# Budgets of the top-k rounds, a parallel first group, spread zero stores and a separate queue for the last gate's stores in a fused attention and expert kernel

## The chip, the cores and the metric

The kernel runs on one core of a Trainium2 chip. The engines are TensorE (PE, with its weight loads PEld), VectorE (DVE), ScalarE (ACT), GpSimd (POOL) and SyncE (SP, which here only issues DMAs); each works through its own instructions in order. The metric is the device time of one execution in microseconds, lower is better.

## What is computed

Attention over 8 batches, 12 heads, 448 positions and head size 64, with q and k normalised by their root mean square, feeds a layer of 8 experts in which every expert keeps its 80 strongest tokens. Cut to what matters:

```python
q_n, k_n = rmsnorm(q, g_q), rmsnorm(k, g_k)      # x / sqrt(mean(x*x) + 1e-6) * g
attn = softmax(q_n @ k_n.T / 8)
x = (attn @ v).transpose(0, 2, 1, 3).reshape(3584, 768)
logits = x @ w_gate                               # 768 x 8
expert_idx, probs = argmax(logits), softmax(logits)
gate_w = probs[arange(N), expert_idx]
for e in range(8):
    tok_idx = where(expert_idx == e)              # the 80 with the largest gate_w
    h = maximum(x[tok_idx] @ w1[e], 0)            # 768 x 1024
    out[tok_idx] = gate_w[tok_idx, None] * (h @ w2[e])   # other rows of out stay zero
```

## The kernel before

**Attention.** The heads are taken in 24 groups of four (three groups to a batch), each group in 7 steps, and two steps make a slot: 84 slots, of about 5 us each, numbered from 0; the slots from -10 prepare the first groups. In a slot PE makes the scores of two steps (L309, and L302 for the 64 left-over positions of each head), ACT takes their exponentials (L311), and PE multiplies those of the slot before with v (L331, L324). DVE adds up the exponentials of a half group in `presum` (L343, L345, L347, L350, all into `sm`), and PE turns the sums and the raw outputs into softmax denominators and gate logits in `zl` (L364, L368), four slots after the group's first. The order of all of this is written out by hand: `at_slot` hangs a step on the beginning, the middle or the end of a slot, and every engine follows that order.

**Preparation of a group.** `load_qk` fetches q and k ten slots ahead on SP's queue, into a ring of five buffers; `square` (ACT, L240), `rstd` (sums on DVE, L249 and L250, then the power -0.5 on POOL, L253), `normalise` (POOL, L263 and L269; DVE for the first two groups) and `transp` (PE, L276 and L281, then the ACT copies L289 and L291) follow. For group 0 this is done in four passes, q and k by two halves each, one pass to a slot from -10 on, each pass whole before the next. Ten matmuls on zeros (`wps`, L810) run on PE ahead of them.

**Gate and top-k.** At the end of batch b, `gate1`, `gate1v`, `gate2` and `gate2b` make the gate weights `gw`, and SP stores them (tile `rg`) to the scratch rows in DRAM, L426 and L429. For batches 0 to 3 together, the 80 best of each expert are found by 10 rounds of DVE's max, index and replace (L475 to L478) on 128 rows of 448 values, and 10 rounds more on 8 rows of 320. The rounds lie in `queue`; at the end of each slot `work(us)` adds its budget to `credit` and takes rounds from the queue while `credit` is above zero, each round charged with `cost`. When the last round is done the token numbers are fetched (`numbers`, POOL), and `close` appends to `first`.

**Merges.** Batches 4 to 7 are ranked in themselves (`rank_in_batch`, L542 to L582) and then merged one after the other into the running 80 best (`merge`): p0 (PE transposes the expert choice, L597, ACT copies it to `eqT`), p1 (PE, L605, with `aval`, ACT copies to `own`), v1 (DVE), p2 (PE, L625, ACT `move`), v2 and v3 (DVE `keep`, `put`), p3 (PE, L651 and L655, ACT `ainfo`), p4 (PE, L663, ACT writes `aval`, which the next merge needs). For batches 4 to 6 `chain_step` hangs these on half slots, no merge before `first` is set; the merge of batch 7 stands behind the loop.

**Zero rows.** 28 stores of zeros to the output (L799) stand on SP's queue, one in each slot from 6 to 33.

**Experts.** Behind the loop SP loads the weights of experts 3 to 5 (L172), POOL gathers the chosen rows (L866), and each expert runs L883, L900, L904, L915, L918 and a scatter (L923). The last batch's `rg` stores stand on SP's queue behind the six weight loads, and the first gather waits for them and for the token numbers `idxT` (L858).

Of the kernel before, what the change touches and what calls it, by code (L numbers as in the profile page):

```python
# [20 lines left out]
def kernel(  # L21
# [50 lines left out]
    nc.scalar.activation(warm[:, 0:1], warm[:, 1:2], AF.Exp)  # L72
# [5 lines left out]
    for half in range(2):  # L78
        nc.scalar.dma_start(out=gk2[half * D:(half + 1) * D, 0:1], in_=g_q[:, None])
        nc.scalar.dma_start(out=gk2[half * D:(half + 1) * D, 1:2], in_=g_k[:, None])  # L80
    gqk = cpool.tile([128, 1], F32, name="gqk")
    nc.vector.tensor_mul(gqk[:, :], gk2[:, 0:1], gk2[:, 1:2])
    nc.vector.tensor_scalar_mul(gqk[:, :], gqk[:, :], 1.0 / math.sqrt(D))
    zsb = cpool.tile([128, 512], F32, name="zsb")
    nc.gpsimd.memset(zsb[:, S:], 1.0)
# [19 lines left out]
    nc.vector.memset(nhalf[:, :], -0.5)  # L105
    ZW = 192
# [79 lines left out]
    with tc.tile_pool(name="qk", bufs=5) as qkpool, \  # L186
# [56 lines left out]
        def rstd(g, a, parts=ALLB):  # L243
# [8 lines left out]
            for lo, hi in parts:  # L252
                nc.gpsimd.tensor_tensor(rs[:, lo:hi], ms[:, lo:hi], nhalf[:, lo:hi], op=ALU.pow)  # L253
# [128 lines left out]
        def gate1v(b):  # L382
# [3 lines left out]
            rg = gpool.tile([128, NT, H + 1], F32, tag="rg", name="rg")  # L386
# [26 lines left out]

        def gate2x(b):
            nc.scalar.activation(gst[b]["lex"][:], gst[b]["lex"][:], AF.Exp)

        def gate2b(b):
# [4 lines left out]
            gw = gpool.tile([128, NT], F32, tag="gw", name="gw", bufs=4)  # L422
            nc.vector.reciprocal(gw[:], lsum[:])
# [5 lines left out]
            nc.sync.dma_start(out=xr_dram[b * S + SM:(b + 1) * S, DM:XW],  # L429
                              in_=rg[:SR, NJ])  # L430
            gwb = gw[:].unsqueeze(2).to_broadcast([128, NT, E])
# [11 lines left out]
        def gate2i(b):  # L443
# [5 lines left out]
            if b == B - 1:  # L449
                nc.gpsimd.memset(info[:], 0.0)  # L450
# [18 lines left out]
        def rounds(get, rows, width, val):  # L469
# [9 lines left out]
            cost = (3 * (width + 60) / 960 + 0.3, )  # L479
# [3 lines left out]
        def lists(val, idx):  # L483
# [9 lines left out]
            return [(0.0, go)]  # L493
# [37 lines left out]
        def rank_in_batch(b, hidden):  # L531
# [53 lines left out]
            return [(0, p1, v1, 4.0), (6, p2, v2, 0.4)]  # L585

        def merge(b, hidden):
# [26 lines left out]
            def v1():  # L614
                m["ahead"] = tpool.tile([128, NT, CAP], BF16, tag="ahead", name="ahead")
                nc.vector.tensor_tensor(m["ahead"][:], m["own"],
                                        m["gw"][:].unsqueeze(2).to_broadcast([128, NT, CAP]),
# [30 lines left out]
            def p3():  # L648
                ps = scps.tile([128, 2, 512], F32, tag="sc", name="mp")
# [105 lines left out]
        for g in range(NG):  # L755
# [24 lines left out]
            if g % NQ == NQ - 1:  # L780
# [8 lines left out]
                if b >= NB0:  # L789
                    at_slot(begins, b0 + 7, gate2i, b)  # L790
# [172 lines left out]
```

## Time and profile before

| | us |
|---|---|
| three runs: median (lowest to highest) | 580.26 (579.28 to 582.1) |
| the profiled execution, its own time | 581.99 |
| its span, first to last instruction | 580.3 |
| PE busy | 506.0 (87%) |
| DVE busy | 340.6 (59%) |
| ACT busy | 313.7 (54%) |
| POOL busy | 297.0 (51%) |

Mean granted clock of TensorE 0.922 of full speed. The shares are means over very different stages: up to about 38 us PE waits for the first groups; from there to about 486 us it works almost without a break, except between 270 and 400 us; from 490 to 530 us it runs at half clock and mostly waits, and then the experts follow. Where PE is busy throughout, work taken off it shortens the time; where it waits, the row that names the releaser tells what would.

### The profile page before, as it was taken

The page shows a single profiled execution, that of the slowest core. Times are in us where ns is not written, and L with a number is a line of the kernel's source. Part 1 is how long each engine was busy: PE and PEld are TensorE (multiplying, and loading weights), DVE is VectorE, ACT ScalarE, POOL GpSimd, SP SyncE. Part 2 cuts the span into 40 slices and gives each one's busy share as a digit, 9 for nine tenths or more (in the row PEclk, how much of TensorE's full clock was granted, in tenths as well). Part 3 has the DMA queues.
Part 4 walks back from the last instruction along what each step waited for, and adds up shares of the span by engine and source line. Part 5 has one row for each costly group of instructions (what it writes and reads, how often), then busy time and mean ns, then how long its engine had stood idle before and what let it go on. Part 6 is the DMA issues. An engine that isn't in the chain of part 4 may idle for free. (4 is left out here: it accounts for less than half of the span.)

```text
span 580.3 us, 9011 instructions
## 1 busy us (share of the span) xinstructions
PE 506.0 (87%) x3325; PEld 228.2 (39%) x3325; DVE 340.6 (59%) x588; ACT 313.7 (54%) x521; POOL 297.0 (51%) x221
## 2 busy tenths in 40 slices
PE   5389999999998999999888999989999998415795
PEld 4133334433333333443223333424435444314674
DVE  2364476464843665379897899494765625502442
ACT  2456776767665676676564664755775633000111
POOL 3479285775955749467175186468781000102231
PEclk8679999999998999999997998999999988556999
DMA  6438989899999969957673496745585500794942
GB/s 168 115 100 168 208 261 219 247 241 255 232 222 275 229 150 198 182 140 157 161 161 77 128 174 125 176 128 89 152 168 89 119 2 32 301 384 129 386 128 69
DMA packets 107531, 100.72 MB, mean 174 GB/s; under 512 B 29152, under 2 KB 99296, under 8 KB 106208
## 3 DMA queue, kind: packets, MB, share of 16 engines
q1 hardware_dynamic: 90736, 70.76, 40.8%
q0 software_dynamic: 15872, 29.14, 28.5%
q8 instruction: 26, 0.43, 0.3%
q10 hardware_dynamic: 880, 0.26, 0.2%
q14 instruction: 17, 0.14, 0.1%
HBM read 101.12 MB, written 39.91 MB: 243 GB/s over the span
## 5 line engine op out<-in xcount | busy, mean ns | idle before, releaser
L253 POOL TENSOR_TENSOR rs<-ms,nhalf 128x14 f32<-128x14 f32 (+2 forms) x52 | 148.6, 2861 | 141.8 <-DVE ms L250 127.9
L311 ACT ACTIVATE at<-ps 128x896 f32<-128x896 f32 x144 | 125.9, 915 | 36.5 <-PE ps L309 18.0
L309 PE MATMUL ps<-qkT 64*128 64x448 f32 x576 | 134.3, 579 | 0.0
L331 PE MATMUL po<-at,vt 128*64 128x448 f32 x576 | 127.3, 557 | 0.0
L249 DVE TENSOR_REDUCE ms<-sq 128x14 f32<-128x896 f32 (+2 forms) x52 | 52.6, 1012 | 87.6 <-ACT sq L240 87.3
L289 ACT ACTIVATE qkT<-tp,gqk 128x448 f32<-128x448 f32 (+2 forms) x72 | 34.1, 508 | 81.3 <-PE tp L281 69.3
L263 POOL TENSOR_TENSOR qn<-qk,rs 128x768 f32<-128x768 f32 x44 | 74.9, 1702 | 0.2
L276 PE MATMUL tp<-ident,qn 128*128 128x128 f32 x288 | 53.8, 297 | 18.9 <-DVE qn L263 16.1
L309 PEld LDWEIGHTS ps<-qkT 64*128 64x128 f32 x576 | 49.3, 189 | 48.3 <-issue 38.4
L343 DVE TENSOR_TENSOR sm<-at 128x896 f32<-128x896 f32 x48 | 57.1, 1189 | 15.1 <-ACT at L311 15.0
L276 PEld LDWEIGHTS tp<-ident,qn 128*128 128x128 f32 x288 | 31.2, 145 | 82.1 <-issue 63.1
L350 DVE TENSOR_TENSOR sm<-sm,at 128x896 f32<-128x896 f32 x48 | 54.7, 1140 | 1.5
L331 PEld LDWEIGHTS po<-at,vt 128*64 128x64 f32 x576 | 34.0, 136 | 54.6 <-issue 52.3
L240 ACT ACTIVATE sq<-qk 128x896 f32<-128x896 f32 (+2 forms) x52 | 46.6, 904 | 3.3 <-DMA gk<-in_g_k_dram 3.3
L364 PE MATMUL zl<-sm,zsel 128*32 128x448 f32 x192 | 33.3, 592 | 11.9 <-DVE sm L350 11.7
L904 ACT ACTIVATE h_sb<-ph 128x320 bf16<-128x320 f32 x16 | 7.0, 437 | 63.3 <-PE ph L900 63.3
L291 ACT COPY qkT<-tp 128x448 f32<-128x448 f32 (+2 forms) x72 | 27.2, 412 | 24.6 <-PE tp L281 24.4
L354 ACT COPY us<-po 128x448 f32<-128x448 f32 x48 | 25.7, 534 | 16.6 <-PE po L324 11.9
L368 PE MATMUL zl<-us,wgs 128*32 128x448 f32 x192 | 33.7, 600 | 0.0
L347 DVE TENSOR_TENSOR sm<-sm,ar 64x896 f32<-64x896 f32 x24 | 30.2, 1258 | 5.4 <-ACT ar L311 4.9
L680 PEld LDWEIGHTS xp<-ident,us 128*128 128x128 f32 x192 | 20.8, 144 | 31.3 <-issue 29.9
L345 DVE TENSOR_TENSOR sm<-sm,ar 64x896 f32<-64x896 f32 x24 | 32.1, 1337 | 0.8
(151 smaller groups left out, 555.2 us busy)
## 6 DMA issues: line engine op xcount, KB each, us to landing
wb_scratch<-in_moe_w_dram POOLq DMA_DIRECT2D x10, 1536.0 KB, 13.9
w_sb<-wb_scratch SPq DMA_DIRECT2D x10, 1536.0 KB, 18.6
out_dram<-zeros SPq DMA_DIRECT2D x28, 384.0 KB, 4.1
vt<-in_v_dram SPq DMA_DIRECT2D x24, 384.0 KB, 7.4
w_sb<-in_moe_w_dram POOLq DMA_DIRECT2D x6, 1536.0 KB, 15.9
xr_scratch<-xb SPq DMA_DIRECT2D x24, 384.0 KB, 4.5
qk<-in_q_dram SPq DMA_DIRECT2D x23, 384.0 KB, 4.6
qk<-in_k_dram SPq DMA_DIRECT2D x23, 384.0 KB, 4.5
```

What stands on the lines that cost most here:

```text
L240: nc.scalar.activation(st[g]["sq%d" % a][:, lo:hi], st[g]["qk"][a][:, lo:hi], AF.Square)
L249: nc.vector.reduce_sum(out=ms[:, lo:hi], in_=st[g]["sq%d" % a][:, lo:hi], axis=AX.X)
L253: nc.gpsimd.tensor_tensor(rs[:, lo:hi], ms[:, lo:hi], nhalf[:, lo:hi], op=ALU.pow)
L263: eng.tensor_mul(qn[:, :M].rearrange("p (j h) d -> p h j d", h=4)[:, h0:h1], qk[:, h0 * NJ:h1 * NJ].rearrange("p (h j) d -> p h j d", j=NJ ...
L276: nc.tensor.transpose(tp[:, j * 128:(j + 1) * 128], qn[:, 4 * j + 2 * u:4 * j + 2 * u + 2].rearrange("p h d -> p (h d)"), ident[:, :])
L289: nc.scalar.activation(o, x, AF.Copy, scale=gqk[:, :])
L309: nc.tensor.matmul(ps[:, hh, :S], T1[d, u, j * 128:(j + 1) * 128], T0[d, u, :], start=True, stop=True)
L311: nc.scalar.activation(at[:], ps[:, :, :S], AF.Exp)
L331: nc.tensor.matmul(st[g]["po%d" % u][hh * D:(hh + 1) * D, :S], vt[:, (2 * u + hh) * NJ + j, :], at[:, hh, :], start=(x == 0), stop=(x == R ...
L343: nc.vector.tensor_add(sm[:], s["at%d" % (x - 1)][:], s["at%d" % x][:])
L350: nc.vector.tensor_add(sm[:], sm[:], s["at%d" % x][:])
L368: nc.tensor.matmul(t[32 * c:32 * c + 32, :S], wgs[:, 4 * i + c, :], st[g]["us%d" % (c // 2)][:, :], start=False, stop=(i == NQ - 1))
```

## The change

Seven edits; the line numbers of the changed kernel are some 5 to 35 higher.

1. Budgets: a round is charged 0.25 us more, `work` adds 2.0 instead of 2.2 us a slot, a ranking is charged 4.6 instead of 4.0, and the gate steps, which were charged nothing, take 2.8 and 1.0 us off the credit (`spent`). A ranking also waits for `listed`, set when the first ten rounds are done and stored.
2. Group 0: both squares, then both `rstd`, then both `normalise` of a half, in three slots; the first half's `rstd` is ACT's square root and DVE's reciprocal instead of POOL's power. The table that holds the exponential is loaded behind it. The gains g_q and g_k are loaded behind k instead of ahead of it. 22 matmuls on zeros instead of 10.
3. Zero stores: from slot 4 on, spread over slots 4 to 78.
4. Buffers: q/k ring 4 instead of 5, `sm` 4 instead of 3, `rg` 4 instead of 2; `gw` is a column of `rg`, which removes a POOL copy.
5. Last gate: its `rg` stores go to ACT's queue; the clearing of `info` on POOL is gone.
6. Last merge: p3 makes only the token number, half as many columns.
7. Matmuls without use (`busy`) on PE ahead of the last merge, behind its p2 and behind its p3: 40, 40 and 70. The clearing of the gather buffers stands further back.

```diff
-    nc.scalar.activation(warm[:, 0:1], warm[:, 1:2], AF.Exp)
+    nc.scalar.activation(warm[:, 0:1], warm[:, 1:2], AF.Sqrt)
...
-    with tc.tile_pool(name="qk", bufs=5) as qkpool, \
+    with tc.tile_pool(name="qk", bufs=4) as qkpool, \
...
             for lo, hi in parts:
-                nc.gpsimd.tensor_tensor(rs[:, lo:hi], ms[:, lo:hi], nhalf[:, lo:hi], op=ALU.pow)
+                if parts is HALF[0]:
+                    nc.scalar.sqrt(rs[:, lo:hi], ms[:, lo:hi])
+                    nc.vector.reciprocal(rs[:, lo:hi], rs[:, lo:hi])
+                else:
+                    nc.gpsimd.tensor_tensor(rs[:, lo:hi], ms[:, lo:hi], nhalf[:, lo:hi],
+                                            op=ALU.pow)
...
-                s["sm%d" % u] = sm = prep.tile([128, 2, S], F32, tag="psm", name="sm", bufs=3)
+                s["sm%d" % u] = sm = prep.tile([128, 2, S], F32, tag="psm", name="sm", bufs=4)
...
+        def spent(us):
+            credit[0] -= us
...
-            nc.gpsimd.tensor_copy(rg[:, :, H], gw[:])
-            nc.sync.dma_start(
+            eng = nc.sync if b < B - 1 else nc.scalar
+            eng.dma_start(
...
-            if b == B - 1:
-                nc.gpsimd.memset(info[:], 0.0)
...
-            cost = (3 * (width + 60) / 960 + 0.3, )
+            cost = (3 * (width + 60) / 960 + 0.55, )
...
-            credit[0] = min(credit[0] + us, us)
+            credit[0] = min(credit[0], 0.0) + us
...
+            if which == "r" and not listed:
+                return False
...
-                        t = -10 + 2 * x + a
+                        t = -10 + 4 * x
                         at_slot(mid, t, square, g, a, HALF[x])
-                        at_slot(mid, t, rstd, g, a, HALF[x])
-                        at_slot(mid, t, normalise, g, a, HALF[x])
+                        at_slot(mid, t + 1, rstd, g, a, HALF[x])
+                        at_slot(mid, t + 2, normalise, g, a, HALF[x])
...
+                at_slot(end, b0 + 6, spent, 2.8)
+                at_slot(end, b0 + 7, spent, 1.0)
...
-            at_slot(begins, 6 + i, lambda i=i: nc.sync.dma_start(
+            at_slot(begins, 4 + 11 * i // 4, lambda i=i: nc.sync.dma_start(
...
-        for i in range(10):
+        for i in range(22):
             nc.tensor.matmul(wps[:, i % 2, :ZW], zeros[:, :128], zeros[:, :], start=True, stop=True)
...
-            work(2.2 if s < NS else 9)
+            work(2.0 if s < NS else 9)
...
+    def busy(n):
+
+        for i in range(n):
+            nc.tensor.matmul(hot[:, :128], identb[:, :], identb[:, :], start=True, stop=True)
...
+    busy(40)
     gate2(b)
```

What the edits move is shown at three places, first DVE at the start, group 0 (`ms` the mean squares, `rs` their inverse roots, `qn` the normalised q or k). Before, q's first half, up to the next pass:

```order
L249 TENSOR_REDUCE ms<-sq 128x6
L250 TENSOR_SCALAR ms<-ms 128x6
L249 TENSOR_REDUCE ms<-sq 128x2
L250 TENSOR_SCALAR ms<-ms 128x2
L119 CAST tabF<-tabI 8x1
L76 CAST identb<-ident 128x128
L263 TENSOR_TENSOR qn<-qk,rs 128x2x3x64
L269 TENSOR_TENSOR qn<-qk,rs 128x128
```

The sums of k begin behind this. Of the change, from the last sum of q's first half on, the same place on DVE:

```order
L254 TENSOR_SCALAR ms<-ms 128x2
L259 RECIPROCAL rs<-rs 128x6
L259 RECIPROCAL rs<-rs 128x2
L253 TENSOR_REDUCE ms<-sq 128x6
L76 CAST identb<-ident 128x128
L123 CAST tabF<-tabI 8x1
L254 TENSOR_SCALAR ms<-ms 128x6
```

k's sums now stand ahead of q's `normalise`, so that q and k go through the chain together.

Second, DVE at the first rounds of top-k, in slot 46 and the slot behind it (`R` the 448 gate weights of a row, `v` the eight largest). Before:

```order
L475 MAX v_162<-R 128x8
L476 MAX_INDEX idx<-v_162,R 128x8
L478 MATCH_REPLACE R<-v_162,R 128x448
L475 MAX v_162<-R 128x8
L476 MAX_INDEX idx<-v_162,R 128x8
L478 MATCH_REPLACE R<-v_162,R 128x448
L343 TENSOR_TENSOR sm<-at 128x896
L350 TENSOR_TENSOR sm<-sm,at 128x896
```

Of the change:

```order
L485 MAX v_156<-R 128x8
L486 MAX_INDEX idx<-v_156,R 128x8
L488 MATCH_REPLACE R<-v_156,R 128x448
L352 TENSOR_TENSOR sm<-at 128x896
L359 TENSOR_TENSOR sm<-sm,at 128x896
```

One round stands in the slot instead of two. By the budgets' arithmetic the twenty rounds take slots 46 to 62 before and 46 to 73 now, `close` comes in slot 81 instead of 70, and the merges of batches 4, 5 and 6 take slots 82 to 90 instead of 71 to 85; the last scores are those of slot 83.

Third, ACT at the end, from the copy of the last batch's logits (`zsb`) to the experts. Before, with the merge of batch 6 in the first rows and that of batch 7 in the last:

```order
L373 COPY zsb<-zl 128x448
L659 COPY ainfo<-mp 80x16
L664 COPY aval<-mp 8x80
L684 COPY xb<-xp 128x4x128
L415 ACTIVATE lex<-lex 128x32
L600 COPY eqT<-mp 8x512
L628 ACTIVATE move<-mp,rowF 80x8
L904 ACTIVATE h_sb<-ph 128x320 x16
```

Of the change, where the merge that ends at the top is batch 4's:

```order
L382 COPY zsb<-zl 128x448
L670 COPY ainfo<-mp 80x16
L675 COPY aval<-mp 8x80
L695 COPY xb<-xp 128x4x128
L610 COPY eqT<-mp 8x512
L621 COPY own<-mp 128x320
L638 ACTIVATE move<-mp,rowF 80x8
...
L427 ACTIVATE lex<-lex 128x32
L610 COPY eqT<-mp 8x512
L438 DMA xr_scratch<-rg 384x1x13
```

Two whole merges (batches 5 and 6) now stand behind the last batch's logits, where none began before.

## Rows read from the trace of the kernel before

**Rows 1.** Waits of PE, whole span: us in total, times, longest
```profile
PE zl L364 <- DVE sm L350: 11.7, 5, 4.6
```

**Rows 2.** Timeline at the start: start us, busy us, engine, line, [idle before <-releaser]
```profile
1.79 6.55 PE L810 MATMUL wps<-zeros 128*128 128x192 f32 x20 [1.79 <-DVE zeros L108]
...
6.24 0.72 ACT L240 ACTIVATE sq<-qk 128x384 f32<-128x384 f32 x2 [3.32 <-DMA gk<-in_g_k_dram]
...
9.06 2.04 POOL L253 TENSOR_TENSOR rs<-ms,nhalf 128x6 f32<-128x6 f32 x2 [5.60 <-DVE ms L250]
...
11.07 0.64 PE L276 MATMUL tp<-ident,qn 128*128 128x128 f32 x3 [2.73 <-DVE qn L263]
...
22.09 3.22 PE L309 MATMUL ps<-qkT 64*128 64x448 f32 x8
...
30.98 0.87 PE L276 MATMUL tp<-ident,qn 128*128 128x128 f32 x3 [4.34 <-DVE qn L263]
```

**Rows 3.** Stretches: length, busy us of each engine, granted clock, DMA share, GB/s
```profile
200.00:250.00 50.00, 49.18 (x300) 19.35 (x298) 26.12 (x35) 35.82 (x57) 25.99 (x17) 1.00 0.87 188
...
300.00:305.00 5.00, 2.10 (x12) 0.35 (x8) 4.76 (x11) 1.89 (x3) 2.61 (x1) 0.99 1.10 208
305.00:310.00 5.00, 3.26 (x13) 0.70 (x14) 4.93 (x9) 0.00 (x0) 2.03 (x1) 0.50 0.92 203
...
350.00:355.00 5.00, 5.00 (x28) 1.34 (x20) 4.83 (x12) 1.57 (x3) 4.32 (x2) 0.73 0.27 69
...
380.00:395.00 15.00, 12.15 (x63) 4.01 (x61) 13.20 (x26) 6.76 (x11) 9.03 (x6) 0.89 0.35 93
```

**Rows 4.** Timeline of DVE, the first two rounds of top-k
```profile
263.96 0.62 DVE L475 MAX8 v<-R 128x8 f32<-128x448 f32 x1
...
266.06 0.63 DVE L475 MAX8 v<-R 128x8 f32<-128x448 f32 x1
```

**Rows 5.** Groups of DVE, 260 to 310 us: count, busy us, mean ns, idle before
```profile
L343 DVE TENSOR_TENSOR sm<-at 128x896 f32<-128x896 f32 x5 | 9.7, 1932 | 0.0
```

**Rows 6.** Timeline at 176 us, ACT
```profile
176.69 0.58 ACT L684 COPY xb<-xp 128x512 f32<-128x512 f32 x1 [2.44 <-DMA xr_scratch<-xb]
```

**Rows 7.** Timeline of PE, steps p1 and p3 of a merge among the attention
```profile
444.72 1.11 PE L605 MATMUL mp<-aval,eqT 8*128 8x80 f32 x8
...
465.98 0.74 PE L651 MATMUL mp<-info,put 128*80 128x16 f32 x8 [0.26 <-ACT at L311]
466.57 1.29 PE L655 MATMUL mp<-ainfo,keep 80*80 80x2 f32 x16
```

**Rows 8.** Timeline of the end, from the last logits to the experts
```profile
484.09 1.28 PE L364 MATMUL zl<-sm,zsel 128*32 128x448 f32 x8
...
486.05 0.32 PE L625 MATMUL mp<-eqb,ahead 128*80 128x8 bf16 x4
...
491.73 0.21 ACT L664 COPY aval<-mp 8x80 f32<-8x80 f32 x1 [0.92 <-PE mp L663]
...
494.40 1.01 PE L597 MATMUL mp<-ident,eq 128*8 128x128 f32 x4 [1.86 <-DVE eq L411]
...
496.07 1.99 PE L605 MATMUL mp<-aval,eqT 8*128 8x80 f32 x8 [0.66 <-ACT eqT L600]
...
496.88 3.09 SPq L172 DMA_DIRECT2D w_sb<-wb_scratch  x6
...
510.17 0.16 DVE L858 CAST idxT<-mp 80x8 uint32<-80x8 f32 x1 [3.52 <-PE mp L655]
...
524.03 1.05 POOL L866 DMA_INDIRECT xg<-xr_scratch,idxT  x1 [24.05 <-DMA xr_scratch<-rg]
...
529.68 3.36 PE L900 MATMUL ph<-xgT,w_sb 128*128 128x80 bf16 x48 [0.50 <-DVE xgT L886]
...
536.04 1.88 PE L900 MATMUL ph<-xgT,w_sb 128*128 128x80 bf16 x48
```

**Rows 9.** Waits of SP's queue, 10 to 480 us: us in total, times, longest
```profile
SPq L204 <- POOL qn L269: 5.0, 3, 3.2
```

More of the change, by code (lines that the diff above doesn't have):

```diff
@@ L77, with load_g, gains @@
     gk2 = cpool.tile([128, 2], F32, name="gk2")
-    for half in range(2):
-        nc.scalar.dma_start(out=gk2[half * D:(half + 1) * D, 0:1], in_=g_q[:, None])
-        nc.scalar.dma_start(out=gk2[half * D:(half + 1) * D, 1:2], in_=g_k[:, None])
     gqk = cpool.tile([128, 1], F32, name="gqk")
[L82 to L85, printed above, removed]
+    def load_g():
+        for half in range(2):
+            nc.scalar.dma_start(out=gk2[half * D:(half + 1) * D, 0:1], in_=g_q[:, None])
+            nc.scalar.dma_start(out=gk2[half * D:(half + 1) * D, 1:2], in_=g_k[:, None])
+    def gains():
+        nc.vector.tensor_mul(gqk[:, :], gk2[:, 0:1], gk2[:, 1:2])
+        nc.vector.tensor_scalar_mul(gqk[:, :], gqk[:, :], 1.0 / math.sqrt(D))
     zsel = cpool.tile([128, NQ, 32], F32, name="zsel")
@@ L105 @@
     nc.vector.memset(nhalf[:, :], -0.5)
+    zsb = cpool.tile([128, 512], F32, name="zsb")
+    nc.gpsimd.memset(zsb[:, S:], 1.0)
     ZW = 192
@@ L385, in gate1v @@
             ztv = zt[:, :].rearrange("p (j c r) -> p j r c", j=NT, c=4)
[L386 removed]
+            rg = gpool.tile([128, NT, H + 1], F32, tag="rg", name="rg", bufs=4)
             rz = rg[:, :, :H].rearrange("p j (i c) -> p j i c", c=4)
@@ L697 @@
         v03 = tpool.tile([128, CAP], F32, name="v03")
-        first, queue, queue2, merging = [], [], [], []
+        first, listed, queue, queue2 = [], [], [], []
         r, ix = rounds(lambda: gst[0]["R"], 128, S, v03)
@@ L797 @@
         at_slot(begins, 0, load_wgs)
+        at_slot(begins, -10, load_g)
+        at_slot(end, -9, gains)
+        at_slot(mid, -8, lambda: nc.scalar.activation(warm[:, 0:1], warm[:, 1:2], AF.Exp))
         for i in range(N // 128):
-            at_slot(begins, 6 + i, lambda i=i: nc.sync.dma_start(
+            at_slot(begins, 4 + 11 * i // 4, lambda i=i: nc.sync.dma_start(
                 out=out[i * 128:(i + 1) * 128, :].rearrange("p (c f) -> p c f", f=ZW),
@@ L838 @@
         fetch_late(e)
-    xgs, xts, gws = {}, {}, {}
-    for e in range(3):
-        xgs[e] = mpool.tile([CAP, XW], F32, tag="xg", name="xg", bufs=3)
-        nc.gpsimd.memset(xgs[e][:, :], 0.0)
+    hot = tpps.tile([128, 512], F32, tag="tp", name="hot")
+    def busy(n):
+        for i in range(n):
+            nc.tensor.matmul(hot[:, :128], identb[:, :], identb[:, :], start=True, stop=True)
     b = B - 1
@@ L854 @@
     rp1()
-    for f in (v1, rv1, p2, rp2, v2, rv2, v3, p3):
-        f()
+    v1()
+    rv1()
+    p2()
+    busy(40)
+    rp2()
+    v2()
+    rv2()
+    v3()
+    p3()
+    busy(70)
     idxT = tpool.tile([CAP, E], U32, name="idxT")
-    nc.vector.tensor_copy(idxT[:, :], gst[B - 1]["out"][:, :, 1])
+    nc.vector.tensor_copy(idxT[:, :], gst[B - 1]["out"][:, :, 0])
     ps_stack.close()
     mps = ctx.enter_context(tc.tile_pool(name="moe_ps", bufs=2, space=PSUM))
+    xgs, xts, gws = {}, {}, {}
+    for e in range(3):
+        xgs[e] = mpool.tile([CAP, XW], F32, tag="xg", name="xg", bufs=3)
+        nc.gpsimd.memset(xgs[e][:, :], 0.0)
     def gather(e):
```

31 lines of the change are left out of this document (16 added, 15 removed).

## Prediction

> **What bounds the kernel now.** I read the waits of PE first, then the stretches, then the timeline where they show a hole. Four parts come out.
>
> At the start PE waits for group 0. The first transposes come at 11.07 us, the first scores at 22.09, and group 1's transposes, behind which PE hardly pauses again, at 30.98, both transposes waiting for DVE's `qn` [rows 2]. q and k pass one after the other through DVE and POOL, whose power alone takes 2.04 us for one pass.
>
> Among the attention PE is the bound: in the stretch from 200 to 250 us it is busy 49.18 of 50, DVE only 26.12 [rows 3]. A slot is then about 5.0 us, my estimate: 84 slots lie between 22.09 and 484.09, 5.5 us each with all stalls. What is taken off PE there, or keeps it from waiting, shortens the time one for one.
>
> With top-k this turns round: from 300 to 310 us DVE is busy 4.76 and 4.93 of 5 and PE only 2.10 and 3.26 [rows 3]. The wait has a name, `zl` for DVE's `sm`, 11.7 us in five waits [rows 1].
>
> At the end a chain: last logits 484.09, `idxT` 510.17, but the first gather only at 524.03, since the last `rg` stores are queued behind six weight loads begun at 496.88 [rows 8]. So 13.7 us of slack lie between `idxT` (done 510.33) and the gather.
>
> **Start: -6 us.** Both squares can begin at 6.24 as now, since ACT issues the same seven DMAs, only in another order. q's sums take 1.1 us and k's as much, four small ACT and DVE operations about 0.2 us each replace POOL's 2.04 us: q and k are both normalised by about 13 us, so the first half is transposed by about 14.5. The second half goes through sums, POOL and `normalise` together: its k is done at about 19.5 and the first scores start at about 19.2, three us early. Group 1 gains more, since its sums no longer stand behind a fourth pass: its transposes come at about 24.5 instead of 30.98. I take -6. Bounds: -7, if all of that moves, and -3, the scores alone. The loading of a second table stands on ACT before it has copies to make and costs nothing as long as DVE's `normalise` covers it; without cover it is one more load ahead of the first copies, inside these bounds. The 22 matmuls on zeros make 44 of what were 20 in 6.55 us [rows 2]; at that pace they would hold PE until 16.2, and if the clock has doubled by the end of the first twenty, until 12. I take the second, because three transposes right behind the twenty took 0.64 us and three of the same at 30.98, after a pause, 0.87 [rows 2], so the twenty had brought the clock up; the first is a rival.
>
> **Budgets: -11 us.** A round takes 2.10 us of DVE (263.96 to 266.06, [rows 4]) and was charged 1.89. At 2.2 us a slot that is 1.17 rounds, 2.45 us, on top of the 2.6 that a slot needs without top-k (26.12 of 50, [rows 3]): 5.05 in a slot of 5.0. DVE can only fall behind. Charged 2.14 at 2.0 a slot it is 0.94 rounds, 1.97 us, 4.57 in all, and the gate's steps are charged too. What goes: PE's idle time, of which 300 to 310 us shows 4.6 us [rows 3] and the waits for `sm` 11.7 [rows 1], and what the fallen clock costs after such a wait: 3.26 us at half clock is 1.6 lost, 5.00 at 0.73 is 1.35, 12.15 at 0.89 is 1.3 [rows 3]. In all 16.0. The stall from 380 to 395 stays, 2.85 idle and 1.3 of clock, because batch 5's gate and ranking stand in the same slots as before; that leaves 11.8, and I take 11. Bounds: -3, if DVE stays near its limit, and -16, if the fourth `sm` buffer covers that stall too.
>
> **Merges that leave the attention: -10 us.** Before, the merges of batches 4 and 5 and the first two steps of 6 ran among the attention; now only the first two steps of 4 do. Two merges of PE work are gone from a stretch in which PE is the bound: p1 1.11, p3 0.74 and 1.29 [rows 7], p2 0.32 [rows 8], p0 and p4 by their cold and later siblings about 0.5 and 0.3: 4.3 us each, 8.5. About 1.5 more for the clock, which falls behind such small matmuls as it does from 350 to 355. Bounds -8 and -10.
>
> **Zero stores: -2.5 us.** At 176.69 ACT waits 2.44 us for the landing of an earlier `xb` store [rows 6], at a time when a zero store goes out in every slot; PE stands still with it. Spread out this should go. Bounds 0 and -3.5 (with a clock that falls).
>
> **End: +6.6 us.** Here the change costs. Count from the last logits, T = 484.09 before. The merge whose p2 stands behind them ends with `aval` at T+7.9 (491.94, [rows 8]). That was batch 6's and is now batch 4's. Two whole merges follow, each needing the `aval` of the one before. One: p0 to the end of p1 3.7 us (494.40 to 498.06), copy and comparison about 1.0 (estimate, two operations of half a us), p2 to `aval` 5.9 (486.05 to 491.94) [rows 8], and half a us because p3 runs cold here: 11.2. Two end at T+30.2. Then 40 useless matmuls on the path: 48 of 80 columns take 3.36 us cold [rows 8], so 40 of 128 about 4.4 (2.5 by the warm row): T+34.6. p0 and its copy 1.7 (494.40 to 496.07). From p1 to `idxT` 14.3 before (496.07 to 510.33); two less, since DVE no longer waits for POOL's clearing and p3 finds the clock up: T+48.4. Before, the gather began at T+39.9. The six loads, begun at T+12.8, have landed by then and so have the `rg` stores, on whichever queue; so the gather is late by 8.5, and what is late next is `idxT` itself. The useless matmuls behind p3 give 1.5 us back at the first expert (3.36 against 1.88) and about 0.4 in its other products. Net +6.6. Bounds: with every merge at full clock (8.4 each, estimate: PE's part halved) -1.5, and +11 if each handover costs some tenths more. Half the columns in p3, one POOL copy less and a strided `gw` are 0.
>
> **Sum.** -6 -11 -10 -2.5 +6.6 = -22.9, against the profiled execution's 581.99: 559.1. That execution lies 1.7 above the median of 580.26, so a median would be at 557.4. I write 558.
>
> **Rivals.** *Forecast*, 558, chance 0.5.
>
> *DVE stays the bound*, 567, 0.2. From 260 to 310 us the five L343 took 1932 ns in the mean, where they take 1.08 elsewhere [rows 5]: one of them is held up whole microseconds while POOL normalises. The Trainium skill ("SBUF — State Buffer", Who interferes with whom) says that a DVE operation with two inputs in SBUF and a POOL operation that reads SBUF exclude one another, the later one blocking fully; by that rule, which this row agrees with, a budget that counts DVE's operations alone is too large. In this stretch the five cost 4.2 us more in 50, 0.4 a slot; with it DVE needs 4.57 + 0.4, again the whole slot, and now for 27 slots instead of 16. Then the -11 shrinks to -2 or -3. Against it: before, by the same count, it was 5.45, so the overload still shrinks from a tenth to nothing.
>
> *The merges at the end run warm*, 550, 0.12. The second and third follow each other without attention between; if the clock holds, the end costs -1.5 instead of +6.6. Against it: the engine waits for ACT and DVE half the time there, as it did from 494 on.
>
> *The zeros hold the first transposes*, 562, 0.13. Without the doubled clock the 44 matmuls end at 16.2, four us too late, and the start gains only 2.
>
> *Slower: four q/k buffers*, 590, 0.05. A load now waits for POOL's `normalise` of the group two before it, which stands only two slots (q) and one slot (k) earlier. SP waited for it three times even with five buffers, 5.0 us [rows 9], and everything on SP's queue waits too. It decides from the point at which POOL runs some 10 us behind its slot, because a load goes out three slots (15 us) before its squares and takes about 5 to land. At 1.5 us of PE a group for 21 groups it is +32 on 558. Against it: POOL's idle time, half of the stretches in [rows 3].
>
> **How the numbers follow.** The range leaves out the slower case and the corner in which all gains are at their bounds: 548 to 572. It takes in the rivals at 550, 562 and 567 and a few us of mistakes in either direction. A measurement of this kernel can tell about 0.5% (2.9 us) from no change. Faster by more 0.88; within 0.5% 0.06, which needs the second rival and an end at its upper bound together; slower 0.06, the last rival and a little.
>
> **What would show it.** Right: the first scores near 19 us and group 1's transposes near 25; PE busy over 4.7 of 5 us where the top-k rounds lie, with waits for `sm` under 4 us besides the one at batch 5's gate; the last logits 29 or 30 us earlier, near 454; from there 48 us to `idxT` at a granted clock of 0.5, and the gather at once behind it. Wrong: waits for `sm` over 10 us; SP waiting for POOL in every group; a gather that still waits for `rg`; less than 42 or more than 55 us from the last logits to `idxT`.

## The result, and the profile after

The changed kernel takes 557.82 us (median of four runs, 555.42 to 559.87) beside 580.14 us for the kernel before on the same chip: a ratio of 0.961, 95% interval 0.956 to 0.966. The prediction was 558. The profiled execution took 559.87 us, its span is 558.0, the mean granted clock 0.946. Medians here and below leave out runs that lie more than 1.5% above the fastest of their kernel.

The waits of PE over the whole span (us in total, times, longest) answer to [rows 1]:

```profile
PE zl L373 <- DVE sm L359: 6.6, 4, 3.3
PE mp L663 <- DVE put L653: 6.5, 4, 2.0
PE tp L285 <- DVE qn L272: 5.5, 3, 4.1
PE pxt L917 <- DVE gws L914: 4.3, 3, 3.4
```

The wait for `sm` has fallen from 11.7 to 6.6 us, not to nothing; the wait for DVE's `put`, a step of the merges, is new in second place.

The start (PE and ACT, answering to [rows 2]):

```profile
1.78 9.69 PE L828 MATMUL wps<-zeros 128*128 128x192 f32 x44 [1.78 <-DVE zeros L112]
...
7.09 1.33 ACT L244 ACTIVATE sq<-qk 128x384 f32<-128x384 f32 x4 [4.24 <-DMA gk<-in_g_q_dram]
8.44 0.21 ACT L258 ACTIVATE rs<-ms 128x6 f32<-128x6 f32 x1
...
11.74 0.52 PE L285 MATMUL tp<-ident,qn 128*128 128x128 f32 x3 [0.27 <-DVE qn L272]
...
18.85 3.36 PE L318 MATMUL ps<-qkT 64*128 64x448 f32 x8
...
24.22 0.53 PE L285 MATMUL tp<-ident,qn 128*128 128x128 f32 x3 [1.18 <-DVE qn L272]
```

First scores 3.2 us earlier, group 1's transposes 6.8 us earlier. The 44 matmuls on zeros end at 11.47 (1.78 + 9.69), just ahead of the first transposes at 11.74.

Where the rounds of top-k lie, in stretches like those of [rows 3] (length, busy us of PE, PEld, DVE, ACT, POOL, granted clock, DMA share, GB/s):

```profile
283.00:288.00 5.00, 3.34 (x18) 0.71 (x14) 4.83 (x10) 2.98 (x4) 2.64 (x2) 1.00 1.09 214
288.00:293.00 5.00, 4.12 (x20) 1.41 (x24) 4.90 (x9) 0.63 (x2) 3.42 (x3) 0.67 1.11 226
...
359.00:374.00 15.00, 12.28 (x65) 4.67 (x67) 14.24 (x30) 7.59 (x13) 7.00 (x6) 0.89 0.52 150
```

DVE is still full there and PE still loses 2.5 us in the ten us of the first two rows; in the worst ten us before it lost 4.6. The last row is batch 5's gate: PE is idle for 2.7 us, 2.85 before.

The end, answering to [rows 8]:

```profile
455.75 1.28 PE L373 MATMUL zl<-sm,zsel 128*32 128x448 f32 x8
...
457.71 0.32 PE L635 MATMUL mp<-eqb,ahead 128*80 128x8 bf16 x4
...
463.85 0.21 ACT L675 COPY aval<-mp 8x80 f32<-8x80 f32 x1 [0.92 <-PE mp L674]
...
475.59 0.21 ACT L675 COPY aval<-mp 8x80 f32<-8x80 f32 x1 [0.39 <-PE mp L674]
...
486.33 4.47 PE L863 MATMUL hot<-identb 128*128 128x128 bf16 x40
486.57 0.21 ACT L675 COPY aval<-mp 8x80 f32<-8x80 f32 x1 [0.39 <-PE mp L674]
...
490.60 0.86 PE L607 MATMUL mp<-ident,eq 128*8 128x128 f32 x4
...
502.02 0.16 DVE L887 CAST idxT<-mp 80x8 uint32<-80x8 f32 x1 [2.20 <-PE mp L666]
502.97 0.98 POOL L900 DMA_INDIRECT xg<-xr_scratch,idxT  x1 [31.96 <-DVE idxT L887]
```

The last logits come 28.3 us earlier. Then two whole merges, 11.7 and 11.0 us from one `aval` to the next, the useless matmuls on the path (4.47), and the last merge; the gather starts right behind `idxT`, 47.2 us after the last logits instead of 39.9. The first expert's first product, which was to gain from the useless matmuls behind p3, takes 1.88 us instead of 3.36.

### The profile page after: what moved, and what is told of

Its sections match the earlier page's. It is cut to its first block, busy times and chain, and to the rows that moved or that the text cites. A ratio compares the mean times of both kernels' runs of the same rounds, so it can differ in the third digit from the quotient of the medians.

```text
span 558.0 us, 9382 instructions
## 1 busy us (share of the span) xinstructions
PE 516.2 (93%) x3499; PEld 243.9 (44%) x3499; DVE 336.0 (60%) x592; ACT 315.8 (57%) x527; POOL 286.0 (51%) x208
## 5 line engine op out<-in xcount | busy, mean ns | idle before, releaser
L261 POOL TENSOR_TENSOR rs<-ms,nhalf 128x14 f32<-128x14 f32 (+1 forms) x48 | 144.4, 3012 | 156.2 <-DVE ms L254 141.8
L318 PE MATMUL ps<-qkT 64*128 64x448 f32 x576 | 132.8, 573 | 0.0
L272 POOL TENSOR_TENSOR qn<-qk,rs 128x768 f32<-128x768 f32 x44 | 70.8, 1608 | 0.2
L298 ACT ACTIVATE qkT<-tp,gqk 128x448 f32<-128x448 f32 (+2 forms) x72 | 34.0, 506 | 62.4 <-PE tp L290 51.2
L352 DVE TENSOR_TENSOR sm<-at 128x896 f32<-128x896 f32 x48 | 54.0, 1124 | 20.3 <-ACT at L320 20.3
L340 PEld LDWEIGHTS po<-at,vt 128*64 128x64 f32 x576 | 34.2, 136 | 55.1 <-issue 54.2
L356 DVE TENSOR_TENSOR sm<-sm,ar 64x896 f32<-64x896 f32 x24 | 32.5, 1354 | 4.8 <-ACT ar L320 4.2
L373 PE MATMUL zl<-sm,zsel 128*32 128x448 f32 x192 | 28.4, 551 | 6.8 <-DVE sm L359 6.6
L691 PE MATMUL xp<-ident,us 128*128 128x128 f32 x192 | 31.9, 289 | 0.6 <-ACT qkT L300 0.6
L695 ACT COPY xb<-xp 128x512 f32<-128x512 f32 x48 | 28.2, 587 | 2.7 <-DMA xr_scratch<-xb 1.4
```

The lines of the kernel that those rows point to most:

```text
L272: eng.tensor_mul(qn[:, :M].rearrange("p (j h) d -> p h j d", h=4)[:, h0:h1], qk[:, h0 * NJ:h1 * NJ].rearrange("p (h j) d -> p h j d", j=NJ ...
L298: nc.scalar.activation(o, x, AF.Copy, scale=gqk[:, :])
L318: nc.tensor.matmul(ps[:, hh, :S], T1[d, u, j * 128:(j + 1) * 128], T0[d, u, :], start=True, stop=True)
L340: nc.tensor.matmul(st[g]["po%d" % u][hh * D:(hh + 1) * D, :S], vt[:, (2 * u + hh) * NJ + j, :], at[:, hh, :], start=(x == 0), stop=(x == R ...
L352: nc.vector.tensor_add(sm[:], s["at%d" % (x - 1)][:], s["at%d" % x][:])
L691: nc.tensor.transpose(xp[:, j * 128:(j + 1) * 128], us[:, c:c + 128], ident[:, :])
```

## The experiments

All kernels in one table. Last logits is the start of the last `zl` (of its second part in `e_fast` and `e_both`, where PE waits between the two parts); the first gather's issue is counted from there, the end from that issue, so that three columns add up, to 0.1 us, to the span of the profiled execution. The medians were measured on several chips; the kernel before took 578.2 to 580.1 there.

| kernel | median us | last logits | first gather behind | to the end |
|---|---|---|---|---|
| before | 580.14 | 484.1 | 39.9 | 56.2 |
| before, again (`b_again`) | 577.56 | 477.9 | 39.4 | 57.1 |
| before, zeros spread (`b_zeros`) | 578.74 | 477.0 | 38.6 | 57.6 |
| after | 557.82 | 455.8 | 47.2 | 55.0 |
| after, again (`after_again`) | 558.18 | 456.3 | 45.9 | 53.7 |
| old budgets (`e_budget_old`) | 561.69 | 471.4 | 24.1 | 64.2 |
| old start (`e_start_old`) | 563.66 | 461.7 | 46.5 | 53.9 |
| old zero stores (`e_zeros_old`) | 559.08 | 456.0 | 45.1 | 52.7 |
| last `rg` stores on SP (`e_rg_sp`) | 556.92 | 455.2 | 47.1 | 53.0 |
| without the first 40 (`e_nobusy1`) | 557.02 | 456.8 | 43.3 | 54.8 |
| shorter chain (`e_chain`) | 552.92 | 457.2 | 39.4 | 54.7 |
| merges early again (`e_fast`) | 561.92 | 470.5 | 26.2 | 64.1 |
| old budgets, loads held back (`e_budget_tie`) | 564.44 | 474.1 | 24.1 | 62.4 |
| merges half early, loads held back (`e_both`) | 557.58 | 463.2 | 30.3 | 62.0 |

**The old budgets.**

```diff
-            cost = (3 * (width + 60) / 960 + 0.55, )
+            cost = (3 * (width + 60) / 960 + 0.3, )
-            work(2.0 if s < NS else 9)
+            work(2.2 if s < NS else 9)
```

(and the other charges of edit 1 as before)

> The changed kernel with the old budgets only (a round charged 0.3 us over its columns, 2.2 us a slot, a ranking 4.0, nothing charged for the gate steps); all else stays changed. My theory: DVE falls behind again while the top-k rounds run and PE waits for sm, over 10 us in all, +8.5; two merges go back into the attention, where PE is the bound, +8; the last logits come at 470 to 474 us instead of 455.75. But then only one and a half merges are left behind them: idxT some 28 us after the last logits instead of 46.4, and the gather at once behind it, while the weight loads are still landing. Net -2, so 553 to 560. First rival: the gather has to share the DMA queues with the weight loads, which landed 39 us after the last logits, and ends no earlier than they do; then only 7 us come back at the end and the time is 565 to 570. Second rival: the stall does not return, since the fourth sm buffer and not the budget took it away; then the last logits come at 464 and the time is 547 to 552.

Measured: 561.69, between the theory and its first rival. From slot 46 to slot 70 (starts of the first scores of a slot) it took 143.3 us, the changed kernel 137.2; from 70 to 83 75.1 instead of 66.7. So the stall is worth 6.1 us and the two merges 8.4; the second rival is out: with a fourth `sm` buffer and the old budgets PE waits 11.5 us for `sm`, as it did with three. The waits of PE and the timeline of the end:

```profile
PE zl L373 <- DVE sm L359: 11.5, 5, 4.7
PE pxt L915 <- DVE gws L912: 9.9, 4, 4.5
```

```profile
471.38 1.28 PE L373 MATMUL zl<-sm,zsel 128*32 128x448 f32 x8
...
484.30 32.96 SPq L176 DMA_DIRECT2D w_sb<-wb_scratch  x10
...
494.51 0.16 DVE L885 CAST idxT<-mp 80x8 uint32<-80x8 f32 x1 [2.88 <-PE mp L666]
495.50 1.04 POOL L898 DMA_INDIRECT xg<-xr_scratch,idxT  x1 [9.04 <-DVE idxT L885]
...
504.20 0.96 DVE L907 TENSOR_TENSOR xn<-xg 80x768 bf16<-80x768 f32 x1 [9.53 <-DMA xg<-xr_scratch,idxT]
```

`idxT` is ready 23.1 us behind the last logits, half of the 46.3 of the changed kernel. But the gather, issued 11 us after the first weight load, takes 8.7 us until DVE uses its rows, and the experts last 64.2 us instead of 55.0. So 15.6 us of attention buy only 3.5 to 4.8 us in the median (beside 557.82 and 558.18 for the changed kernel and 556.92 with `rg` on SP).

What fills the time is seen in the DMA share, the last column but one. With the early gather the DMA engines are full from the loads on; in the changed kernel they stand still before its gather, the first six loads being done:

```profile
494.00:505.00 11.00, 6.72 (x74) 6.54 (x73) 0.96 (x2) 0.00 (x0) 2.98 (x3) 0.76 1.02 371
...
515.00:525.00 10.00, 8.19 (x130) 6.79 (x128) 4.15 (x8) 1.75 (x4) 2.89 (x3) 1.00 1.00 383
```

```profile
495.00:503.00 8.00, 6.69 (x85) 6.60 (x84) 4.88 (x16) 0.00 (x0) 0.03 (x1) 0.71 0.01 2
```

**Are the loads the cause?** Only the two loads of expert 3 go out early; the other eight wait behind the first gathers.

```diff
     for e in range(3):
         gather(e)
+    nc.sync.dma_start(out=tie_dram[:, :], in_=xgs[2][:1, :8])
+    for e in range(NW0 + 1, NW0 + 3):
+        fetch_late(e)
```

> The old budgets as in the first of these kernels, and besides only the two weight loads of expert 3 go out before the gathers; the other eight wait, by a 32-byte copy of the third gathered tile on SP's queue, until the first three gathers have landed. With the old budgets alone the time from the first gather's issue to the end was 64.2 us instead of 55.0, and PE waited 9.9 us for gathered rows instead of 4.3. Theory: the gathers share the queues with the weight loads, and that alone is the 9 us; with the loads behind them it is 55 to 58 again, and the time 554 to 557. Rival: the experts are late for another reason, or now wait for their weights: 62 us or more, and no gain over 561 to 563.

Measured: 564.44, no gain. The waits of PE, and the timeline:

```profile
PE pxt L916 <- DVE gws L913: 10.6, 4, 4.0
```

```profile
498.17 1.05 POOL L899 DMA_INDIRECT xg<-xr_scratch,idxT  x1 [9.44 <-DVE idxT L886]
...
501.90 0.95 DVE L908 TENSOR_TENSOR xn<-xg 80x768 bf16<-80x768 f32 x1 [4.54 <-DMA xg<-xr_scratch,idxT]
...
505.01 8.69 SPq L177 DMA_DIRECT2D w_sb<-wb_scratch  x8
...
537.33 0.95 DVE L908 TENSOR_TENSOR xn<-xg 80x768 bf16<-80x768 f32 x1 [4.08 <-DMA xg<-xr_scratch,idxT]
```

Both sides hold in part. The first gather is quick again (3.7 us instead of 8.7), so it was the loads that held it up: the Trainium skill ("DMA: Bandwidth & Descriptors", Queues, rings and completion order) says that each DMA engine goes round between the queues that have work for it, and these two rows agree. But the later gathers now wait for rows, four waits of up to 4.0 us, and 62.4 us is close to 64.2. Holding the loads back moves the wait to a later gather, and the DMA engines are as full then, only later:

```profile
515.00:525.00 10.00, 7.33 (x86) 5.51 (x85) 3.06 (x6) 1.31 (x3) 1.91 (x2) 0.87 1.01 387
```

That it is the traffic as a whole which takes this time, whenever the gathers come, fits these rows; no run left weights out, so it is argued and not shown.

**Merges early without the stall.** The two kernels put merges back into the attention while a round and a ranking keep their new charges; the gate steps are no longer charged.

```diff
-            todo = [(0.0, place), stop, stop, (0.0, turn), stop]
+            todo = [(0.0, place), stop, (0.0, turn), stop]
...
-                if e % 3 == 2:
+                if e == 3:
...
-            return [(0, p0, None, 0), (1, p1, v1, 1.0), (4, p2, v23, 1.7), (4, p3, None, 0),
+            return [(0, p0, None, 0), (1, p1, v1, 1.0), (2, p2, v23, 1.7), (2, p3, None, 0),
...
-                at_slot(end, b0 + 6, spent, 2.8)
-                at_slot(end, b0 + 7, spent, 1.0)
```

(the edit of the first; both contain the shorter chain below; the second has four pauses ahead of `close`, steps three half slots apart, and the loads held back. A pause is a `stop` in the list of steps, which ends what a slot may take from it.)

> As the kernel with the shorter chain, and besides: five pauses fewer where the token numbers are fetched, merge steps two half slots apart instead of four, and the gate steps not charged, so that the merges of batches 4 and 5 and half of 6 lie in the attention again. Theory: 8.6 us of PE work go back into the attention and DVE costs some 2 us more, so the last logits come near 466; idxT then 18 to 20 us behind them, but its gathers share the queues with the weight loads and the experts take about 64 us from the first gather as they did with the old budgets, instead of 55: 549 to 553, much the same as the shorter chain alone. Rival: the experts are not held up by the loads but by something of the old budgets: 542 to 545.

> The shorter chain, the gate steps not charged, one pause fewer before the transposes, the fetches in two groups of four with four pauses behind them, merge steps three half slots apart, and the weight loads held back until the first gathers have landed. Theory: merge 4 and the first steps of 5 go into the attention (+6 us of PE work), DVE no longer stands at the fetched numbers (it stood 9.0 us with two pauses), so the last logits come at 462 to 464; two and a half merges follow: idxT 28 to 31 us behind them, experts 55 us: 547 to 551, 2 to 5 us under the shorter chain alone. Rival: the PE work and DVE waits that go back into the attention cost as much as the end gains: 552 to 556.

The first expectation says five pauses fewer; the edit leaves five of seven, so it takes out two. Measured: 561.92 and 557.58, worse than the shorter chain by itself and slower than the theory and the rival of either expectation. In the first, `close` comes too early behind the fetches. Waits around 414 to 428 us, and the timeline of DVE and POOL:

```profile
DVE ainfo L532 <- DMA num<-tab_scratch,add: 9.0, 1, 9.0
...
PE ps L319 <- ACT own L622: 5.2, 1, 5.2
```

```profile
416.88 1.46 POOL L273 TENSOR_TENSOR qn<-qk,rs 128x768 f32<-128x768 f32 x1
417.17 2.99 DVE L532 TENSOR_TENSOR ainfo<-num,bad 80x8 f32<-80x8 uint32 x1 [8.99 <-DMA num<-tab_scratch,add]
...
418.67 1.46 POOL L273 TENSOR_TENSOR qn<-qk,rs 128x768 f32<-128x768 f32 x1
```

DVE stands 9.0 us at numbers that POOL had fetched late; behind it stand a gate and ACT's copy `own`, and behind that the scores, 5.2 us of PE. The experts take 64.1 and 62.0 us from the first gather, with the new charges as with the old: what they wait for hangs on how early the first gather is against the loads, not on the budgets. The kernel before fits this too: merges of two batches lie in its attention, but its gather comes 27 us behind the first load, and its experts take 56.2.

Up to slot 70 these two kernels are the faster ones: slots 46 to 70 take 134.1 and 134.4 us instead of 137.2, and the longest wait for `sm` of the changed kernel (3.3 us, see below) is not there. Of their edits only the missing charge for the gate steps acts so early, so this part of edit 1 costs some 2 to 3 us (the shorter chain, which keeps it, takes 136.1); no run takes it out alone.

**The last `rg` stores back on SP's queue.**

```diff
-            eng = nc.sync if b < B - 1 else nc.scalar
+            eng = nc.sync
```

> The changed kernel with the last gate's stores back on SP's queue, behind the six weight loads. Theory: nothing, 557 to 559, since those loads land 39 us after the last logits and idxT comes only 46 us after them; the gather starts at once behind idxT as now. Rival: the stores land later than idxT (before, they took 23.0 us behind the loads): then the gather waits for rg and the time rises by 1 to 5 us.

Measured: 556.92; the gather (issued at 502.3 us) waits for `idxT` and not for the stores. The separate queue is worth nothing here, since the merges now hide the stores. With the merges early it should matter: with the old budgets and the separate queue the gather comes 24.1 us behind the last logits, while in the two profiles of the kernel before `idxT` was nearly as early (26.1 and 25.3) and the gather came at 39.9 and 39.4, waiting for `rg` [rows 8]. No run changes the queue alone with early merges, so what it is worth in time there is open.

**The old start.** Group 0 in four passes, POOL's power, the gains first, ten matmuls.

```diff
-                        t = -10 + 4 * x
+                        t = -10 + 2 * x + a
...
-        for i in range(22):
+        for i in range(10):
```

> The changed kernel with the old start: group 0 in four passes one after the other, POOL's power for every half, the gains loaded ahead, ten matmuls on zeros, the table of the exponential from the beginning. The slot starts of the two traces differ by 7.7 us from slot 5 on, so the theory says +7.7 +-1 (565.5), with the first scores near 22 and group 1's transposes near 31 us. Rival: part of the 7.7 comes from the other edits at the start (fewer zero stores beside the first loads, the smaller q/k ring); then +5 or less.

Measured: 563.66, 5.5 to 6.7 above the changed kernel (557.82 and 558.18) and the one with `rg` on SP (556.92). Its slot 7 begins at 58.9 us, against 52.7 in the first profile of after, but 53.7 in the second. That is less than the theory's 7.7 +-1 but for the largest of the three differences, and more than the rival's 5. The slots decide: 58.9 lies among the 60.4 and 58.6 of the kernel before and the 59.2 of that with the zeros spread, which have the larger q/k ring besides, so no part is seen for the other edits; 7.7 was the size of one pair of profiles.

**The changed kernel again.** No edit.

> The changed kernel once more, unchanged, beside the others on one chip. Theory: 556 to 560 as before. In its first profile the scores of slot 3 began at 32.9 us, in other kernels with the same start at 34.6 to 36.1, and TensorE's clock rose at once at 24.2 us in the one and up to 5 us later in the others; if that is chance, this profile lies between 32.9 and 36.1 in slot 3. Rival: the start of the other kernels was late because of their edits; then 32.9 again.

Measured: 558.18; slot 3 begins at 34.6. So chance; and the kernel with `rg` on SP, which does have an edit, began it at 33.0. The rows to see it in are the first product with v and the stretch that it takes (the last column but two is the granted clock), in the first profile of after and in that of the shorter chain, whose start is the same code:

```profile
26.65 1.72 PE L340 MATMUL po<-at,vt 128*64 128x448 f32 x8
26.65:28.37 1.72, 1.72 (x13) 0.55 (x10) 1.69 (x4) 1.70 (x3) 0.19 (x1) 1.00 0.71 185
```

```profile
28.91 2.66 PE L341 MATMUL po<-at,vt 128*64 128x448 f32 x8
28.91:31.57 2.66, 2.66 (x13) 0.84 (x10) 1.03 (x2) 1.75 (x2) 2.66 (x1) 0.64 0.58 161
```

The same eight matmuls, at full clock in the one and mostly at half clock in the other: the clock rose some us later behind the same wait, and slot 3 began at 32.9 in the one and 36.1 in the other.

**The zero stores, from both sides, and the kernel before again.**

```diff
-            at_slot(begins, 4 + 11 * i // 4, lambda i=i: nc.sync.dma_start(
+            at_slot(begins, 6 + i, lambda i=i: nc.sync.dma_start(
```

(in the changed kernel; the reverse in the kernel before)

> The changed kernel with the 28 zero stores back in slots 6 to 33. Theory: ACT waits again for the landing of an xb store while they go out, +3.6 us (561.5), all of it between slots 28 and 33, with a wait of xb over 2 us there. Rival: with the other edits the loads and stores stand apart anyway, or slack behind takes it back: under +1.

> The kernel before with only the zero stores spread over slots 4 to 78. From slot 28 to slot 31 the kernel before took 18.9 us and the changed kernel 15.3, but the changed kernel with the stores put back took 15.3 too. First theory (my prediction): the spread stores take the stall away here, 15.3 in this stretch and 3 us off the whole, 576 to 577. Second theory: something else of the change took it away, the stretch stays near 18.9 and the time within 1 us of the kernel before. Third: the stall comes and goes from execution to execution; then this stretch says nothing by itself, and the runs of this kernel lie closer together than those of the kernel before.

> The kernel before once more, unchanged. In its first profile the stretch from slot 28 to slot 31 took 18.9 us; with the zero stores spread it took 15.5, but in the changed kernel 15.3 with the stores in either place. If the stall belongs to the kernel before, 18 to 19 again here and the zero stores are its cause there; if it comes and goes, about 15.5, and the 3.6 us that the two first profiles show in this stretch are no effect of the edit.

From slot 28 to slot 31: before 18.9 us, before again 15.7, before with zeros spread 15.6, after 15.3, after with the old stores 15.3. In the second profile of before the ACT wait of [rows 6] is

```profile
173.41 0.59 ACT L684 COPY xb<-xp 128x512 f32<-128x512 f32 x1 [0.82 <-DMA xr_scratch<-xb]
```

0.82 us instead of 2.44, with nothing edited. So the 3.6 us between the two first profiles come and go without the edit; whether spread stores make them rarer, these few profiles can't tell. In time, the spread gains 0.3% in the kernel before (ratio 0.997, interval 0.9935 to 1.0005), and putting the stores back gives 559.08 (three runs, 555.55 to 560.61) beside 556.92 for the kernel with `rg` on SP in the same comparison. An effect of 1 or 2 us is possible; none is shown.

**The chain at the end.** First without the forty matmuls ahead of the last merge, then with each following merge's p0 placed where PE waits for `put`.

```diff
     rp1, rv1, rp2, rv2 = rank_in_batch(b, False)
-    busy(40)
```

```diff
+            steps = [x + (b, ) for x in merge(b, True)]
+            if merges:
+                merges.insert(len(merges) - 2, steps.pop(0))
+            merges.extend(steps)
...
-    busy(40)
```

(the first `busy` alone; the last batch's p0 and gate steps go into the loop too)

> The changed kernel without the first forty useless matmuls (those ahead of the last merge). First theory: they only stand in the way; p0 of the last merge follows aval at once, 4.5 us earlier, its p1 runs cold (1.99 instead of 1.11), the second forty still bring the clock up before p3: idxT 3 to 4 us earlier, 554 us. Rival: without them the clock is still down when p3 runs (1.22 and 2.27 instead of 0.74 and 1.51) and at the first expert (3.36 instead of 1.88), and the gain is under 1 us.

> The changed kernel without the first forty useless matmuls and with the p0 of every merge but the first moved ahead of the p3 of the merge before it, where PE waits for DVE's put; the last batch's gate steps go into the loop. Theory: the serial chain behind the last logits sets the end; each of the three p0 with its copy takes 1.5 us off it and the forty matmuls 3 to 4, so idxT comes 38 to 39 us after the last logits instead of 46.4 and the time is 549 to 551. Rival: the weight loads, which land 39 us after the last logits, hold up the first gather, and it lands 4 us later after its issue than now: 553 to 555.

Measured: without the forty, the gather comes 43.3 us behind the last logits instead of 45.9 to 47.2; the last p1 then takes 1.99 us instead of 1.11 and the last p3 0.90 and 2.27 instead of 0.74 and 1.51, so part is given back, as the rival says. The median of 557.02 can't be told from 557.82. With the shorter chain the gather comes at 39.4 and the time is 552.92 us (548.75 to 554.31), between the theory and the rival; the ratio to before is 0.949, interval 0.940 to 0.958. It is the fastest kernel here, all its runs below all eight of the changed kernel (555.42 to 559.87). Its timeline:

```profile
464.41 0.21 ACT L676 COPY aval<-mp 8x80 f32<-8x80 f32 x1
...
474.07 0.21 ACT L676 COPY aval<-mp 8x80 f32<-8x80 f32 x1 [0.39 <-PE mp L675]
...
483.79 0.21 ACT L676 COPY aval<-mp 8x80 f32<-8x80 f32 x1 [0.39 <-PE mp L675]
484.06 1.99 PE L616 MATMUL mp<-aval,eqT 8*128 8x80 f32 x8 [0.30 <-ACT aval L676]
...
495.60 0.16 DVE L894 CAST idxT<-mp 80x8 uint32<-80x8 f32 x1 [2.15 <-PE mp L667]
496.54 0.98 POOL L907 DMA_INDIRECT xg<-xr_scratch,idxT  x1 [26.33 <-DVE idxT L894]
```

A merge now takes 9.7 us from `aval` to `aval` instead of 11.0 to 11.7, and the last one's p1 follows `aval` at once (484.06; in the changed kernel 5.6 us later). The experts take 54.7 us, as with a later gather: this one comes 28 us after the loads began (468.06).

## Why the prediction was right

The time is right, and so is the mechanism of the start, the merges and the end; but one term had no cause behind it and one was mis-sized. The two first profiles, and the two second ones (the kernel before and after again), give for each term:

| term | predicted | first pair | second pair | undone alone, in time |
|---|---|---|---|---|
| start (slot 7) | -6 (-7 to -3) | -7.7 | -5.0 | 5.5 to 6.7 |
| budgets (46 to 70) | -11 (-16 to -3) | -8.5 | -7.5 | 6.1 by slots |
| merges out of the attention (70 to 83) | -10 (-10 to -8) | -8.0 | -8.4 | 8.4 to 9.0 by slots |
| zero stores (28 to 31) | -2.5 (-3.5 to 0) | -3.6 | -0.3 | not told from 0 |
| end (from the last logits) | +6.6 (-1.5 to +11) | +6.0 | +3.1 | |
| span | -22.9 | -22.3 | -18.5 | |

Budgets and merges together, undone, cost 3.5 to 4.8 us in time, the earlier end included. What is missing from a column's sum to its span lies between the places named.

- **Start: right.** Both squares, the small operations in place of POOL's power, first scores near 19 (18.85) and group 1's transposes near 24.5 (24.22) came as worked out. The first half is transposed at 11.74 and 13.30, earlier than the 14.5 predicted, and nothing waits on it. The -7.7 of the first pair lies beyond the bound of -7; the second pair shows how much of that was chance. The rival of the zeros fell: 44 matmuls take 9.69 us where twenty took 6.55, so the 24 added ones cost some 3.1 us, where the pace of the first twenty would have made it 7.9.
- **Budgets: mechanism right, size off.** The step that failed is the count of DVE in a slot, 4.57 of 5.0. Over slots 46 to 56, where the first ten rounds lie, DVE is busy 57.0 us, 5.2 a slot:

```profile
246.24:308.45 62.21, 59.54 (x344) 22.77 (x342) 56.97 (x97) 39.18 (x64) 33.77 (x23) 0.97 0.76 177
```

  Two things are missing from the 4.57, the second of them priced as a rival. A slot without top-k takes 2.9 us of DVE, not 2.6, when a gate lies among the slots counted (32.4 us in slots 32 to 42). And five additions that ran beside POOL's `normalise` took 4.8 us longer than the shortest of their shape, 0.4 a slot. With the rounds' 1.7 a slot this makes 5.0 of the 5.2. So PE was busy 4.72 of 5 in the mean of slots 46 to 73, just over the 4.7 named, but 3.34 and 4.12 in the worst ten us, and the waits for `sm` are 6.6 us, where "under 4 besides the gate" was named. None of them is at the gate: 2.5 us lie among the rounds of the first ten, and the longest, 3.3, where the second ten begin. There DVE waits for POOL's copy of the rows, and then has a round and the ranking of batch 4 (L565 to L570) ahead of the sums for which PE waits. The rows are these:

```profile
320.74 0.48 DVE L485 MAX8 aval<-canda 8x8 f32<-8x320 f32 x1 [3.28 <-POOL canda L502]
...
324.61 0.29 DVE L565 TENSOR_SCALAR beat<-row,rg 128x128 bf16<-128x128 f32 x1
...
327.25 0.28 DVE L570 SCALAR_TENSOR_TENSOR tied<-row,rg,tri 128x64 bf16<-128x64 f32 x1
...
329.78 0.57 PE L373 MATMUL zl<-sm,zsel 128*32 128x448 f32 x2 [3.34 <-DVE sm L359]
```

  A charge in the budget doesn't know of that wait for POOL. The rival of DVE held up by POOL, 567, had its mechanism right, and its 0.4 a slot is what was measured: a half-height addition (L356) takes up to 2.82 instead of 1.08 us beside POOL's `normalise`. Only its price is wrong: the stall shrank by 6.1 to 8.5 us, not by 2 or 3.
- **Merges: the lower bound.** -8.0 to -8.4 against 8.5 of PE work counted; the 1.5 us for the clock, which were added on top, did not appear.
- **Zero stores: wrong.** The -2.5 seemed confirmed by the first pair of profiles. The step that failed is the first: a wait of 2.44 us that stood once in one execution was taken for a property of the kernel. That execution lay near the top of its kernel's runs (581.99 in 579.28 to 582.1), and the second profile has 0.82 us in that place.
- **End: right.** Merges of 11.7 and 11.0 us against 11.2 worked out, forty useless matmuls 4.47 against 4.4, half clock in both of them (granted clock 0.5 from 460.4 to 491.1; p1 1.99, p3 1.22 and 2.27), the gather right behind `idxT`, `idxT` 46.3 us behind the last logits against 48.4. The rival of warm merges fell. The parts named for one merge add up to 11.1, not 11.2, which changes nothing. What the prediction didn't ask is what an early gather would be worth: the experts take 53 to 58 us when the gather comes 27 us or more behind the first load, and 62 to 64 when it comes 11 or 12 us behind, or when the loads wait for it.
- **Four q/k buffers:** SP waits for POOL's `normalise` 7.0 us in five waits, instead of 5.0 in three. But PE waits for `qn` only at the start, the last time at 24.22; the rival is out.

So the sum came out right partly by luck: errors of either sign cancelled. The gains of budgets, merges and zero stores were forecast too large by 2.5 to 3.5, by 1.6 to 2 and by up to 2.5 us, the end too dear by 0.6 to 3.5, and the start was 1.7 too small by the first pair and 1.0 too large by the second.

## What to carry to other kernels

Serial work can be cheap behind the stage in which an engine is the bound, as long as a transfer that must be waited for anyway runs beside it; so ask first how long that transfer is, and put just as much of the chain there. Then shorten that chain: a step that doesn't need the previous result (here the transposes of the next merge) belongs in a wait of the step before. And a stall that stands once in one trace is an event, not a property: look for it in a second profile of the same kernel before it gets a term in the sum.

## What the runs showed of the hardware

- The same code after the same wait of PE for DVE met either level of TensorE's clock. In the first profile of after, group 1's first transposes took 0.53 us at 24.22 with a granted clock of 1.00 from 24.2 to 26.0; in that of the shorter chain 0.87 us at 24.40, with 0.50 from there to 28.9. In the second profile of after the clock was up at 24.3, fell at 25.6 and rose again at 29.0. In the ten profiles with this start slot 7 began at 52.7 and 52.8 us where the clock was up from 23.5 on, at 53.7 to 53.9 where it rose for good between 28 and 29, and at 55.1 where it rose at 30.8: up to 2.4 us hang on it.
- DVE's addition of 80x8 elements took 2.99 us, from 417.17 to 420.16, with POOL's `normalise` running beside it until 420.13. The Trainium skill ("SBUF — State Buffer", Who interferes with whom) says that the two share a port pair under an exclusive lock; the rows agree, and show that one small operation can sit through two of POOL's large ones.
- A gather of 80 rows landed so that DVE could start 3.6 us after its issue (502.97 to 506.59 in the changed kernel) with the first six weight loads done (DMA share 0.01 ahead of it), and 8.7 us with them under way (495.50 to 504.20 with the old budgets, DMA share 1.02).
